# Retention and top-1 MoE on one core: expert 0's rows transposed inside the last retention tiles, expert 1's weight splits on two engines, its x transposed later, x loads tied to TensorE

## The chip, the core and the metric

The kernel runs on one core of one Trainium2 chip. The metric is the device time of one execution in microseconds (us). Runs of the kernel before: 649.43 us median of 3 (648.3 to 650.15).

Engines are called PE (TensorE; PEld is its weight load), DVE (VectorE), ACT (ScalarE), POOL (GpSimd) and SP (SyncE, which here only issues DMAs). "Clock" is the granted TensorE clock as a share of full speed.

## The reference

```python
# attention: 8 batches, 8 heads, 576 positions, head size 64
scores = (q @ k.T) / sqrt(64)
ret = scores * Dmat               # gamma_h ** (i - j) for i >= j, else 0; no softmax
x = (ret @ v)                     # -> [4608, 512], one row per token
# mixture of experts, top 1 of 8, F = 1024
logits = x @ w_gate
e_idx = argmax(logits, axis=1)
gate_w = softmax(logits)[e_idx]
eom = sigmoid(x @ w_output_gate)
for e in range(8):
    rows = e_idx == e
    h = relu(x[rows] @ w1[e])     # [., 512] @ [512, 1024]
    out[rows] = gate_w[rows] * eom[rows, e] * (h @ w2[e])
```

## The kernel before

**Phase 1, the retention.** 36 tiles of 128 tokens (`NTILE`), g = 0 to 35. Per tile PE makes the scores (L317), transposes k (`k_rows`, PSUM tile `k_ps`, L300), turns the last tile's result into row blocks with the gate logits (`xnat`, L437, tiles `xa`, `xb`), makes the tile's output (`outT`, L348 and L351, tile `o_ps`) and updates the state (`update`, L333, tile `st_ps`). DVE masks the scores (L319), adds the logits (L448, L449) and scales the output into `xT` (L355). Every fourth tile the gate runs: `gate1` on DVE (argmax, softmax, counts), `gate2` on PE (ranks, L394, L395), `gate3` on DVE (slots). Then POOL scatters the rows by indirect DMA into a DRAM buffer `xs` with a region for each expert (L185), and fills the unused slots of each region (`fill`, from `zx`). During this phase the weights of expert 0 are loaded (`start_w`), rounded by ACT (`hi_w`, L137) and the remainder taken by DVE (`lo_w`, L142) by the table `wsched`. Every operand of the MoE is split into such a high and a low part, and a product is three matmuls: high with high, high with low, low with high.

**Phase 2, the experts.** Each expert has 616 slots: part 0 with 360 (tiles 0 to 2, of 128, 128 and 104 rows) and part 1 with 256 (tiles 3 and 4, starting at slot 360). `mm1(e, part, fb)` makes one of eight h groups of a part: 12 matmuls (L237) into `h_ps`, of 360 or 256 columns, then ACT's `hh` (L239) and DVE's `hl` (L240). `mm2(e, t)` makes one tile of y: 24 matmuls (L253), then ACT's scaled copy (L256) and POOL's indirect store (L257). Expert 0 runs part 0 first as a whole (all h groups, then y of tiles 0 to 2) and then part 1; the other experts interleave the two parts group by group.

**How x reaches PE.** Expert 0's tiles 0 to 2 are loaded as rows (`load_rows`, one DMA of 2 KB rows, tile `x_g`) at g = 32 and transposed on PE (`transp`, L218) into `h_ps` after the retention. All other tiles are loaded by `load_x` (four DMAs of 128 pieces of 512 bytes, tile `x_q`, five buffers) and transposed in blocks by DVE (L221, tile `x_t`). In both cases ACT then rounds (`xh`, L223) and DVE takes the remainder (`xl`, L224). Every read of `xs` waits for all scatters and fills that were issued ahead of it in the program (`scat`, in `read`, L154).

**What sets the order.** The program is written in a fixed order (`manual_schedule`), and each engine runs its instructions in that order. Between the phases only PE, ACT, DVE and SP are fixed (`every`, L473, L510). SP has one queue, for all loads of weights, x and indices. From expert 1 on, the weights are split by DVE alone (`load_w`, L146 and L147); for expert 1 this happens during expert 0's part 1, where DVE also transposes expert 1's tiles 1 and 2; tile 0 is done ahead of it, tiles 3 and 4 with the last two y groups. The short POOL memsets on `gap` stand between scatters.

Of the kernel before, what the change touches and what calls it, by code (L numbers as in the profile page):

```python
# [47 lines left out]
def tile_retention_moe(  # L48
# [101 lines left out]
    XG, XT, HT = {}, {}, {}  # L150
    scat, todo, at = [], [], {}
    pools = {"xt0": xta, "ht0": hpa}

    def read(**kw):  # L154
        i = SP.dma_start(**kw)
        for j in scat:
            tc.add_manual_dep(i.ins, j.name, SYNC, reason="reads the rows after every scatter so far")
        tc.add_to_no_dep_group("xs", i.ins)
# [6 lines left out]
    def load_x(e, t):  # L165

        XG[e, t] = pools["xq"].tile([P, 4, P], F32, name="x_q")
        o = e * NT + ROW0[t]
        for a in range(4):
            read(out=XG[e, t][32 * a:32 * a + 32],  # L170
                 in_=xs[o:o + P, P * a:P * a + P].rearrange("(u j) c -> j u c", u=4))
# [35 lines left out]
    def transp(e, t):  # L207
# [7 lines left out]
        if e == 0 and part == 0:  # L215
            src = pools["ps_h"].tile([P, KB, P], F32, name="h_ps")[:, :, 0:m]
            for k in range(KB):
                T.transpose(src[:, k, :], XG[e, t][0:m, k:DM:KB], ident[0:m, 0:m])  # L218
        else:
            src = pools["xq"].tile([P, KB, P], F32, name="x_t", bufs=2)  # L220
            V.transpose(out=src.rearrange("p k (u j) -> p u k j", u=4),  # L221
                        in_=XG[e, t].rearrange("p u (i k) -> p u k i", k=KB))
# [3 lines left out]
    def mm1(e, part, fb):  # L226
# [8 lines left out]
        for k in range(KB):  # L235
            for a, b in ((wh, xh), (wh, xl), (wl, xh)):
                T.matmul(ps, lhsT=a[:, k, :], rhs=b[:, k, 0:n], start=(j == 0), stop=(j == 3 * KB - 1))  # L237
                j += 1
# [3 lines left out]
    def mm2(e, t):  # L242
# [6 lines left out]
        for fb in range(FB):  # L249
            wh, wl = (a[:, fb % 2, :] for a in W2[e, fb // 2])  # L250
            hh, hl = HT[e, part, fb]
            for a, b in ((hh, wh), (hh, wl), (hl, wh)):
                T.matmul(ps, lhsT=a[:, n], rhs=b, start=(j == 0), stop=(j == 3 * FB - 1))  # L253
                j += 1
# [217 lines left out]
    gap = const.tile([1, 1], F32, name="gap")  # L472
    every = {mybir.EngineType.PE, mybir.EngineType.Activation, mybir.EngineType.DVE, mybir.EngineType.SP}  # L473
    with tc.manual_schedule():
        S_next = scores(0)
        k_rows(0)
        for g in range(NTILE):
# [13 lines left out]
            if g + 1 < NTILE:  # L491
                prep(g + 1)
                S_next = scores(g + 1)
                k_rows(g + 1)
            if todo and g >= GT * SNAP + 10:
# [5 lines left out]
            update(g)  # L501
            if g % GT == 0 and g > 0:
# [8 lines left out]
    rest.__enter__()  # L511
    xnat(NTILE - 1)
    gate1(NTILE // GT - 1)
    for t in range(TA):
        transp(0, t)
# [50 lines left out]
    mm1(0, 0, 0)  # L566
# [12 lines left out]
    mm1(0, 0, 1)  # L579
    rest.__exit__(None, None, None)  # L580
    gap_ = gap

    def fill_slots(e):
        for f in fills[e]:
            G.memset(gap_, 0.0)
# [3 lines left out]
    for t in range(TA, CT):  # L589
        load_x(0, t)  # L590
    load_idx(0, 1)
    fill_slots(1)
    for t in range(3):
        load_x(1, t)
    load_idx(1, 0)
    load_idx(1, 1)
    fill_slots(2)
    for fb in range(2, FB):
        mm1(0, 0, fb)
    for t in range(TA):  # L600
        mm2(0, t)
        if t < CT - TA:
            transp(0, TA + t)
        else:
            transp(1, 0)
    for e in range(E):
        nx = e + 1 < E
        for fb in range(FB):
# [5 lines left out]
            if nx:  # L614
                if fb < CT if e else fb in (2, 3):
                    load_x(e + 1, fb if e else fb + 1)
                if e and fb in (5, 6):
# [3 lines left out]
            if fb == 7 and e + 3 < E:  # L621
                fill_slots(e + 3)
            if e == 0 and fb in (2, 6):
                transp(1, 1 if fb == 2 else 2)
        if e == E - 1:
            overflow_table()
        for t in range(CT):
            if e > 0 or t >= TA:
                if nx:
                    transp(e + 1, t)  # L630
# [99 lines left out]
```

## Time and profile before

| what | before |
|---|---|
| runs, median of 3 | 649.43 us (648.3 to 650.15) |
| the profiled execution, its time | 650.73 us |
| its span, from the first to the last instruction | 648.9 us |
| mean granted clock over the span | 0.982 |
| PE busy | 621.5 us (96%) |
| DVE busy | 358.7 us (55%) |
| ACT busy | 170.8 us (26%) |
| POOL busy | 166.9 us (26%) |
| bytes moved by DMA | 96.24 MB, mean 148 GB/s |

A row of the profile names the line of the kernel, the engine and the operation, then output and inputs by the program's names, then the shape and the count. In a view by time the first two numbers are the start and the duration in us; the brackets at the end hold the engine's idle time ahead of the instruction and what ended it. In a view by stretch each engine's busy time stands with its count of instructions, then the clock, the share of the DMA engines' time and the rate in GB/s. A busy PE is not PE at its peak: matmuls are pipelined, and their ends are modelled.

### The profile page before, as it was taken

To read this page: it belongs to the slowest core of one execution; us is meant where nothing else is said; L and a number is where in the kernel's file an instruction comes from. 1 tells how busy PE (TensorE), PEld (TensorE's weight loads), DVE (VectorE), ACT (ScalarE), POOL (GpSimd) and SP (SyncE) were. 2 spreads that over 40 slices of the span, in tenths; PEclk is the share of its full clock that TensorE was granted. 3 is DMA by queue.
4 is the path that set the end of the run, shared out by engine and by line. 5 is a ranking of instruction groups with operands and counts; after the bars stand their busy time and mean duration, and the time that the engine had idled before them with its cause. 6 is when DMAs were issued, how large, how long until landed. Compare 5 with 4: busy or idle time off the path is not lost. (4 is left out here: it accounts for less than half of the span.)

```text
span 648.9 us, 12779 instructions
## 1 busy us (share of the span) xinstructions
PE 621.5 (96%) x5127; PEld 551.9 (85%) x5127; DVE 358.7 (55%) x750; ACT 170.8 (26%) x379; POOL 166.9 (26%) x229
## 2 busy tenths in 40 slices
PE   8999999989969699999999999999999999999995
PEld 6888888878859488997997898799799889979974
DVE  3567787677753237773575286267438518625420
ACT  2333433323431122222222222222222222222210
POOL 2244433545426441401501320150110110010011
PEclk9999999989989699999999999999999999999999
DMA  9867686656424545633364183254417416311001
GB/s 323 275 232 251 219 292 231 215 197 240 147 90 129 141 138 162 188 106 127 115 178 130 59 235 88 82 151 117 143 62 212 126 36 186 123 46 65 0 34 43
DMA packets 55610, 96.24 MB, mean 148 GB/s; under 512 B 14736, under 2 KB 36625, under 8 KB 55548
## 3 DMA queue, kind: packets, MB, share of 16 engines
q1 hardware_dynamic: 45836, 72.99, 37.1%
q0 software_dynamic: 9280, 21.36, 9.0%
q10 hardware_dynamic: 432, 1.05, 0.4%
q8 instruction: 41, 0.67, 0.4%
q14 instruction: 21, 0.17, 0.1%
HBM read 74.02 MB, written 30.64 MB: 161 GB/s over the span
## 5 line engine op out<-in xcount | busy, mean ns | idle before, releaser
L237 PE MATMUL h_ps<-xh,w1h 128*128 128x360 f32 (+1 forms) x512 | 157.1, 307 | 2.9 <-ACT xh L223 2.5
L237 PE MATMUL h_ps<-xl,w1h 128*128 128x360 f32 (+1 forms) x512 | 157.0, 307 | 0.3 <-DVE xl L224 0.3
L237 PE MATMUL h_ps<-xh,w1l 128*128 128x360 f32 (+1 forms) x512 | 156.9, 306 | 0.0
L253 PE MATMUL y_ps<-w2h,hh 128*128 128x512 f32 (+1 forms) x320 | 127.2, 397 | 4.8 <-ACT hh L239 4.8
L257 POOL DMA_INDIRECT out_dram<-y,idx x40 | 39.7, 994 | 346.8 <-ACT y L256 333.8
L253 PE MATMUL y_ps<-w2h,hl 128*128 128x512 f32 (+1 forms) x320 | 126.4, 395 | 1.5 <-issue 1.5
L253 PE MATMUL y_ps<-w2l,hh 128*128 128x512 f32 (+1 forms) x320 | 126.4, 395 | 0.0
L240 DVE SCALAR_TENSOR_TENSOR hl<-h_ps,hh 128x360 fp32r<-128x360 f32 (+1 forms) x128 | 58.7, 475 | 101.1 <-ACT hh L239 99.3
L237 PEld LDWEIGHTS h_ps<-xh,w1h 128*128 128x128 f32 x512 | 97.7, 191 | 3.6 <-ACT xh L223 2.7
L239 ACT ACTIVATE hh<-h_ps 128x360 fp32r<-128x360 f32 (+1 forms) x128 | 54.9, 429 | 171.0 <-PE h_ps L237 151.1
L237 PEld LDWEIGHTS h_ps<-xl,w1h 128*128 128x128 f32 x512 | 97.7, 191 | 1.0 <-DVE xl L224 0.7
L237 PEld LDWEIGHTS h_ps<-xh,w1l 128*128 128x128 f32 x512 | 97.5, 190 | 0.0
L253 PEld LDWEIGHTS y_ps<-w2h,hh 128*128 128x128 f32 (+1 forms) x320 | 59.5, 186 | 20.6 <-ACT hh L239 6.2
L224 DVE TENSOR_TENSOR xl<-x_t,xh 128x512 fp32r<-128x512 f32 x37 | 25.6, 692 | 91.1 <-ACT xh L223 90.4
L253 PEld LDWEIGHTS y_ps<-w2h,hl 128*128 128x128 f32 (+1 forms) x320 | 59.5, 186 | 16.5 <-issue 1.3
L253 PEld LDWEIGHTS y_ps<-w2l,hh 128*128 128x128 f32 (+1 forms) x320 | 59.5, 186 | 14.4
L256 ACT ACTIVATE y<-y_ps,idx 128x512 f32<-128x512 f32 (+1 forms) x40 | 27.6, 690 | 146.7 <-issue 77.2
L319 DVE TENSOR_TENSOR S_sb<-sc,cmat_sb 128x512 f32<-128x512 f32 x72 | 46.1, 682 | 17.9 <-PE sc L317 17.9
L185 POOL DMA_INDIRECT xs<-xgrp,sli x36 | 38.3, 1063 | 66.8 <-ACT xgrp L443 20.9
L306 POOL TENSOR_TENSOR vp<-pk,gk_sb 128x512 f32<-128x512 f32 x36 | 37.6, 1044 | 54.0 <-PE st_ps L333 40.5
L185 POOL DMA_INDIRECT xs<-zx,fill x40 | 47.2, 1180 | 9.5 <-issue 9.4
L317 PE MATMUL sc<-pk 64*128 64x128 f32 x576 | 43.7, 289 | 1.8 <-DVE S_sb L319 1.5
(116 smaller groups left out, 669.9 us busy)
## 6 DMA issues: line engine op xcount, KB each, us to landing
st<-in_w_dram SPq DMA_DIRECT2D x64, 512.0 KB
pk<-in_pack_dram SPq DMA_DIRECT2D x32, 768.0 KB
x_q<-xs SPq DMA_DIRECT2D x148, 64.0 KB
gq_sb<-in_gq_dram SPq DMA_DIRECT2D x5, 256.0 KB
pk<-in_pack_dram SPq DMA_DIRECT2D x4, 256.0 KB
pk<-in_pack_dram SPq DMA_DIRECT2D x2, 512.0 KB
xs<-zx,fill POOLq DMA_INDIRECT x40
out_dram<-y,idx POOLq DMA_INDIRECT x40
```

The lines of the kernel that those rows point to most:

```text
L185: i = G.indirect_dma_start(out=xs, out_offset=bass.IndirectOffsetOnAxis(ap=at, axis=0), in_=x, in_offset=None, **({} if bound is None else ...
L224: V.tensor_tensor(out=lo, in0=src, in1=hi.bitcast(F32), op=ALU.subtract)
L237: T.matmul(ps, lhsT=a[:, k, :], rhs=b[:, k, 0:n], start=(j == 0), stop=(j == 3 * KB - 1))
L239: A.activation(out=hh, in_=ps, func=AF.Relu)
L240: V.scalar_tensor_tensor(out=hl, in0=ps, scalar=0.0, in1=hh.bitcast(F32), op0=ALU.max, op1=ALU.subtract)
L253: T.matmul(ps, lhsT=a[:, n], rhs=b, start=(j == 0), stop=(j == 3 * FB - 1))
L256: A.activation(out=y, in_=ps, func=AF.Copy, scale=idx.bitcast(F32)[0:m, e, t, 1:2])
L257: G.indirect_dma_start(out=out, out_offset=bass.IndirectOffsetOnAxis(ap=idx[0:m, e, t, 0:1], axis=0), in_=y, in_offset=None, bounds_check= ...
L306: G.tensor_tensor(out=vs[g], in0=pk[g][:, 2].rearrange("p (h d) -> p h d", h=H), in1=gk_sb[:, g % CPB].broadcast_to([P, H, D]), op=ALU.mult)
L317: T.matmul(sc[r][:, p], lhsT=k, rhs=q, start=True, stop=True)
L319: V.tensor_tensor(out=S_sb[:, r], in0=sc[r], in1=m, op=ALU.mult)
```

## The change

- `transp` for expert 0 uses PE for all five tiles, into a PSUM tile that `pools["ps_x"]` names: `k_ps` in the retention, `t_ps` later. Tiles 0 and 1 are transposed in iterations g = 34 and 35, after `scores(g + 1)` and ahead of `xnat(g - 1)`, tile 2 after the last `outT`.
- `mm1(0, 0, 0)` goes ahead of `xnat(35)` and the last `gate1`, and `mm1(0, 0, 1)` ahead of `gate2`.
- Expert 0's tiles 3 and 4 are loaded as rows, and transposed on PE between y of tile 1 and y of tile 2.
- Expert 1's first weights: the loads of quarters 0 and 1 are issued right after expert 0's last x, those of 2 and 3 in part 1; the split is ACT's `hi_w` and DVE's `lo_w` in two halves each instead of DVE alone.
- Expert 1's x: tile 0 is loaded behind y of tile 1, tile 1 behind the transposes and y of tile 2, tiles 2 to 4 at h groups 1, 3 and 5 of part 1. The first DMA of each also waits for the first matmul of the group that was last written in the program (`pe[0]`). All five are transposed at the end: 0 to 2 ahead of y of tile 3, 3 and 4 ahead of y of tile 4.
- The slot fills of expert 2 move from the start of phase 2 into part 1 of expert 0, the later ones from three experts ahead to two.

```diff
+    pe = [None]
-    def read(**kw):
+    def read(paced=False, **kw):
         i = SP.dma_start(**kw)
+        if paced:
+            tc.add_manual_dep(i.ins, pe[0].name, SYNC, reason="not before TensorE is at this point")
...
-            read(out=XG[e, t][32 * a:32 * a + 32],
+            read(paced=e == 1 and a == 0, out=XG[e, t][32 * a:32 * a + 32],
...
-        if e == 0 and part == 0:
-            src = pools["ps_h"].tile([P, KB, P], F32, name="h_ps")[:, :, 0:m]
+        if e == 0:
+            src = pools["ps_x"].tile([P, KB, P], F32, name=pools["x_ps"])[:, :, 0:m]
...
+            if g >= NTILE - 2:
+                transp(0, g - NTILE + 2)
...
             update(g)
+            if g == NTILE - 1:
+                transp(0, 2)
...
+    mm1(0, 0, 0)
     xnat(NTILE - 1)
     gate1(NTILE // GT - 1)
-    for t in range(TA):
-        transp(0, t)
...
-    mm1(0, 0, 0)
+    pools["ps_x"], pools["x_ps"] = ps_t, "t_ps"
+    mm1(0, 0, 1)
     gate2(ps_t.tile([P, 512], F32, name="t_ps"), True)
...
-    mm1(0, 0, 1)
...
     for t in range(TA, CT):
-        load_x(0, t)
+        load_rows(0, t)
     load_idx(0, 1)
+    w = [start_w(1, 1, fp) for fp in range(2)]
     fill_slots(1)
-    for t in range(3):
-        load_x(1, t)
+    for fb in range(2, FB):
+        mm1(0, 0, fb)
     load_idx(1, 0)
     load_idx(1, 1)
-    fill_slots(2)
-    for fb in range(2, FB):
-        mm1(0, 0, fb)
-    for t in range(TA):
-        mm2(0, t)
-        if t < CT - TA:
-            transp(0, TA + t)
-        else:
-            transp(1, 0)
+    mm2(0, 0)
+    mm2(0, 1)
+    load_x(1, 0)
+    for t in range(TA, CT):
+        transp(0, t)
+    mm2(0, 2)
+    load_x(1, 1)
...
-            if nx:
-                if fb < CT if e else fb in (2, 3):
-                    load_x(e + 1, fb if e else fb + 1)
-                if e and fb in (5, 6):
+            if e == 0:
+
+                if fb in (0, 2):
+                    w.append(start_w(1, 1, 2 + fb // 2))
+                if fb in (1, 3, 5):
+                    load_x(1, 2 + fb // 2)
+                if fb % 2 == 1:
+                    hi_w(*w[fb // 2])
+                    lo_w(*w[fb // 2])
+            elif nx:
+                if fb < CT:
+                    load_x(e + 1, fb)
+                if fb in (5, 6):
...
-            if fb == 7 and e + 3 < E:
-                fill_slots(e + 3)
-            if e == 0 and fb in (2, 6):
-                transp(1, 1 if fb == 2 else 2)
+            if fb == (7 if e else 4) and e + 2 < E:
+                fill_slots(e + 2)
...
             if e > 0 or t >= TA:
-                if nx:
-                    transp(e + 1, t)
+                for u in (t,) if e else range(3) if t == TA else range(3, CT):
+                    if nx:
+                        transp(e + 1, u)
                 mm2(e, t)
```

On PE, at the end of the retention (state update of tile 34, row block, output of tile 35), the order was, with the numbers of buffers in the names:

```order
L333 MATMUL st_ps<-vp,kn 64x64 x8
L437 MATMUL xa<-iw,xT 128x144 x2
L437 MATMUL xb<-iw,xT 128x144 x2
L348 MATMUL o_ps<-pk,stT_95 64x128 x8
L351 MATMUL o_ps<-S_sb,vp 64x128 x8
L437 MATMUL xa<-iw,xT 128x144 x2
L437 MATMUL xb<-iw,xT 128x144 x2
L218 MATMUL h_ps<-cmat_sb,x_g 128x128 x8
L218 MATMUL h_ps<-cmat_sb,x_g 128x104 x4
L237 MATMUL h_ps<-xh_2797,w1h_572 128x360
```

At the same place the changed kernel has (its line numbers are higher by 3 to 12):

```order
L340 MATMUL st_ps<-vp,kn 64x64 x8
L221 MATMUL k_ps<-cmat_sb,x_g 128x128 x4
L444 MATMUL xa<-iw,xT 128x144 x2
L444 MATMUL xb<-iw,xT 128x144 x2
L355 MATMUL o_ps<-pk,stT_95 64x128 x8
L358 MATMUL o_ps<-S_sb,vp 64x128 x8
L221 MATMUL k_ps<-cmat_sb,x_g 128x104 x4
L240 MATMUL h_ps<-xh_2673,w1h_572 128x360
```

The transposes stand between the pieces of the last tiles, and the first h group follows the last output directly; the last `xa` and `xb` come after its 12 matmuls.

On SP, from the last weights of expert 0 on, the queue was:

```order
L128 DMA st<-in_w_dram 128x1024
L155 DMA x_q<-xs 32x4x128 x8
L155 DMA idx<-xs 128x2x2
L155 DMA x_q<-xs 32x4x128 x12
L155 DMA idx<-xs 128x3x2
L155 DMA idx<-xs 128x2x2
L128 DMA st<-in_w_dram 128x1024
L155 DMA x_q<-xs 32x4x128 x8
L128 DMA st<-in_w_dram 128x1024 x4
```

and it is now:

```order
L128 DMA st<-in_w_dram 128x1024
L156 DMA x_g<-xs 128x512 x2
L156 DMA idx<-xs 128x2x2
L128 DMA st<-in_w_dram 128x1024 x2
L156 DMA idx<-xs 128x3x2
L156 DMA idx<-xs 128x2x2
L156 DMA x_q<-xs 32x4x128 x8
L128 DMA st<-in_w_dram 128x1024
L156 DMA x_q<-xs 32x4x128 x4
L128 DMA st<-in_w_dram 128x1024
```

Two row loads stand in place of the first eight x pieces, two weight loads come ahead of expert 1's x, and the x pieces come by four with weights between them.

On DVE, at the end of expert 0's part 1 (the last h groups, then the border to expert 1), the order was:

```order
L221 STREAM_TRANSPOSE x_t<-x_q 128x4x4x32
L224 TENSOR_TENSOR xl_3193<-x_t,xh_3192 128x4x128
L240 SCALAR_TENSOR_TENSOR hl_3354<-h_ps,hh_3353 128x256
L146 CAST w1h_3372<-st 128x1024
L147 TENSOR_TENSOR w1l_3373<-st,w1h_3372 128x1024
L221 STREAM_TRANSPOSE x_t<-x_q 128x4x4x32
L224 TENSOR_TENSOR xl_3397<-x_t,xh_3396 128x4x128
L221 STREAM_TRANSPOSE x_t<-x_q 128x4x4x32
L224 TENSOR_TENSOR xl_3397<-x_t,xh_3396 128x4x128
```

and it is now:

```order
L245 SCALAR_TENSOR_TENSOR hl_3350<-h_ps,hh_3349 128x256
L142 TENSOR_TENSOR w1l_3242<-st,w1h_3241 128x512 x2
L224 STREAM_TRANSPOSE x_t<-x_q 128x4x4x32
L227 TENSOR_TENSOR xl_3371<-x_t,xh_3370 128x4x128
L224 STREAM_TRANSPOSE x_t<-x_q 128x4x4x32
L227 TENSOR_TENSOR xl_3371<-x_t,xh_3370 128x4x128
L224 STREAM_TRANSPOSE x_t<-x_q 128x4x4x32
L227 TENSOR_TENSOR xl_3371<-x_t,xh_3370 128x4x128
L224 STREAM_TRANSPOSE x_t<-x_q 128x4x4x32
L227 TENSOR_TENSOR xl_3415<-x_t,xh_3414 128x4x128
L224 STREAM_TRANSPOSE x_t<-x_q 128x4x4x32
L227 TENSOR_TENSOR xl_3415<-x_t,xh_3414 128x4x128
```

All five tiles of expert 1 (`xl_3371` is its part 0, `xl_3415` its part 1) now stand in one row behind the last weight split.

## Prediction before the run

> **What bounds the kernel now.** I read the page's busy line first, then busy time by stretch over the change of phase, then TensorE (PE) in order of time with the idle time ahead of each piece, then what released ScalarE (ACT) and VectorE (DVE) there.
>
> ```profile
> PE 621.5 (96%) x5127; PEld 551.9 (85%) x5127; DVE 358.7 (55%) x750; ACT 170.8 (26%) x379; POOL 166.9 (26%) x229
> ```
>
> PE is busy 96% of the span of 648.9 us, and the change takes no matmul away, so a gain can only come from its 27.4 us of idle time and from time at a reduced clock. The stretches (columns: us, then busy time of PE, PEld, DVE, ACT, POOL, then the granted clock) show where both lie:
>
> ```profile
> 182.40:185.80 3.40, 1.72 (x14) 1.75 (x15) 2.12 (x5) 0.75 (x2) 0.38 (x2) 1.00 0.30 113
> 185.80:189.30 3.50, 0.97 (x9) 0.80 (x8) 3.12 (x16) 1.81 (x5) 0.00 (x0) 1.00 0.01 2
> 189.30:196.10 6.80, 6.52 (x23) 5.87 (x24) 2.37 (x11) 1.50 (x3) 0.00 (x0) 0.50 0.00 0
> 196.10:208.70 12.60, 12.60 (x78) 12.60 (x77) 5.19 (x17) 2.36 (x5) 9.23 (x12) 1.00 0.43 147
> ...
> 213.10:216.60 3.50, 0.91 (x3) 0.48 (x3) 0.53 (x1) 0.47 (x1) 2.93 (x6) 1.00 0.76 182
> 216.60:226.80 10.20, 6.50 (x16) 4.84 (x16) 3.25 (x4) 1.67 (x3) 1.97 (x2) 0.50 0.57 148
> ```
>
> There are two holes: around 182 to 196 us (the last retention tile, the transposes of expert 0's rows, its first h groups) and 213 to 227 us (the first y group). Each is followed by a stretch at clock 0.50. PE in order of time, first hole:
>
> ```profile
> 178.81 0.73 PE L437 MATMUL xa<-iw,xT 128*128 128x144 f32 x4 [0.85 <-DVE xT L355]
> ...
> 180.56 1.09 PE L351 MATMUL o_ps<-S_sb,vp 128*64 128x128 f32 x16
> 184.08 0.73 PE L437 MATMUL xa<-iw,xT 128*128 128x144 f32 x4 [2.43 <-DVE xT L355]
> ...
> 185.14 1.58 PE L218 MATMUL h_ps<-cmat_sb,x_g 128*128 128x128 f32 x12
> 189.25 0.67 PE L237 MATMUL h_ps<-xh,w1h 128*128 128x360 f32 x1 [2.53 <-ACT xh L223]
> 190.20 0.67 PE L237 MATMUL h_ps<-xl,w1h 128*128 128x360 f32 x1 [0.28 <-DVE xl L224]
> ```
>
> Second hole, and its end where the first 256-column group starts:
>
> ```profile
> 206.62 0.33 PE L237 MATMUL h_ps<-xh,w1l 128*128 128x360 f32 x1
> ...
> 208.75 0.39 PE L253 MATMUL y_ps<-w2h,hh 128*128 128x512 f32 x1
> 214.14 0.50 PE L253 MATMUL y_ps<-w2h,hh 128*128 128x512 f32 x1 [1.05 <-ACT hh L239]
> 216.43 0.48 PE L253 MATMUL y_ps<-w2h,hl 128*128 128x512 f32 x1 [1.55 <-issue]
> 220.61 0.79 PE L253 MATMUL y_ps<-w2h,hh 128*128 128x512 f32 x1 [3.70 <-ACT hh L239]
> ```
> ```profile
> 235.33 0.28 PE L237 MATMUL h_ps<-xh,w1h 128*128 128x256 f32 x1
> ```
>
> In the second hole PE waits for hh of groups 6 and 7, which ACT makes late, and ACT itself says why:
>
> ```profile
> 213.62 0.47 ACT L239 ACTIVATE hh<-h_ps 128x360 fp32r<-128x360 f32 x1 [8.08 <-remote]
> 220.09 0.47 ACT L239 ACTIVATE hh<-h_ps 128x360 fp32r<-128x360 f32 x1 [6.00 <-remote]
> ```
>
> Group 6 ends on PE at 206.62 + 0.33 = 206.95, yet ACT, idle and waiting for PE alone, starts 6.7 us later; group 7 ends near 208.92 and is taken 11.2 us later. "Remote" says that the release was not tied to an instruction at that time. What ran meanwhile is on the queues: SyncE's reads of expert rows in 512-byte pieces.
>
> ```profile
> 206.04 4.40 SPq L155 DMA_DIRECT2D x_q<-xs  x8
> 210.49 0.43 SPq L155 DMA_DIRECT2D idx<-xs  x1
> 212.76 7.47 SPq L155 DMA_DIRECT2D x_q<-xs  x12
> ```
>
> Both late releases fall into these issues, the second at the end of the burst. That the burst holds them up is my reading, not a row.
>
> **Part A: the transposes move into the retention, one h group goes ahead of the last row block (PE).** Before, PE left the retention's last matmul at 180.56 + 1.09 = 181.65 and reached y at 208.75. After, on the same clock of time: VectorE gets one xl (0.6 us; the three of them take 1.78) ahead of xT(34), for which PE already waits (0.85), so the tail ends some 0.55 later, at 182.2; the other transposes there fill that wait. Then the third tile's transposes, 4 of the 12 that took 1.58: 0.5. Their cast and subtraction are now exposed: about 0.75 until xh and 0.45 until xl, 1.2. Then 8 h groups of 12 at 12.60/77 = 0.164 (the window's 78 hold one that began before): 15.7. The last row block, 184.08 to 185.14: 1.05. The rank matmuls and a short wait for DVE's counts: 0.5. Sum 182.2 + 0.5 + 1.2 + 15.7 + 1.05 + 0.5 = 201.2, so A = 208.75 - 201.2 = **7.55 us** saved. The new group 0 covers xT(35) and group 1 covers the gate's chain on DVE. Bounds: if DVE's xT(35) is released late again (2.43 idle in its row) and the clock halves again, 7.55 - 1.6 - 3.0 = 3; if the casts hide wholly, 8.7.
>
> **Part B: expert 0's last two tiles and expert 1's x.** The whole-row load of tiles 3 and 4 is 2 issues instead of 8, and expert 1's x no longer follows in the same burst: 12 of the 20 x_q issues wait for PE's first y groups or later. The last scatters move with the gate. Before (rows below), the rank matmuls came at 193.67, the first scatter at 197.17, the first read at 206.04. The rank matmuls now come after h group 1, at 182.2 + 0.5 + 1.2 + 2 x 1.97 + 1.05 = 188.9 or a little later, 4.5 earlier, so the reads come near 201.5, just after h group 7 has ended. So the late releases should go.
>
> ```profile
> 193.67 0.25 PE L394 MATMUL t_ps<-oh,cbf_sb 128*128 128x32 bf16 x1
> ```
> ```profile
> 197.17 1.26 POOL L185 DMA_INDIRECT xs<-xgrp,sli  x1 [14.39 <-issue]
> ```
>
> What is late next? The transposes of tiles 3 and 4, which PE meets after two y groups:
>
> ```profile
> 246.80:257.80 11.00, 11.00 (x50) 9.06 (x49) 8.77 (x12) 2.67 (x5) 0.98 (x1) 1.00 0.69 191
> ```
>
> That stretch holds two undisturbed y groups, 48 matmuls, and an h record at each edge: 10.97, or 0.2285 each. So PE is at the transposes at 201.2 + 10.97 = 212.2. The loads are 512 KB; at the 182 GB/s of the window 213.1 to 216.6 they take 2.9 us, at a third of it 8.6, so they are there by 204.4 to 210.1. Their cast and subtraction (1.2 and 1.4) lie under the third y group. B: before, 208.75 to 235.33 = 26.58; after, 72 x 0.2285 = 16.45 and 8 transposes at 1.58/12 = 0.13, 1.05. B = 26.58 - 17.5 = **9.1 us** saved, so PE is at the 256-column groups at 218.7. Bounds: 0 if the releases stay late, 10 if the transposes hide.
>
> **Part C: x of expert 1 after its weights (VectorE, then PE).** The weight splits themselves go from DVE alone (0.69 + 1.23 each) to ACT and DVE; per two 256-column groups ACT has 2 x 0.39 + 1.14 and DVE 2 x 0.42 + 1.28 of work in 2.88 us of PE, so both keep up. But all five tiles of x(1) are now transposed in one chain after the last split:
>
> ```profile
> 253.69 1.08 DVE L221 STREAM_TRANSPOSE x_t<-x_q 128x512 f32<-128x512 f32 x1
> 255.52 0.69 DVE L224 TENSOR_TENSOR xl<-x_t,xh 128x512 fp32r<-128x512 f32 x1 [0.74 <-ACT xh L223]
> 256.13 1.08 DVE L221 STREAM_TRANSPOSE x_t<-x_q 128x512 f32<-128x512 f32 x1
> ```
> ```profile
> 178.33 1.14 ACT L137 CAST w2h<-st 128x512 fp32r<-128x512 f32 x2
> ```
>
> One tile takes 256.13 - 253.69 = 2.44, since DVE waits for ACT's cast in between. Count from the end of the last 256-column group: hh 0.55, the last weight cast 1.14, the second half of its subtraction 0.7: the chain starts at 2.4. The fifth xl starts at 2.4 + 4 x 2.44 + 1.83 = 14.0 and ends at 14.7; its xh is there at 14.0. PE has 10.97 of y and 12 x 0.164 = 1.97 of h(1,0,0) until it needs tiles 3 and 4 at 12.94. Before, the last two tiles were done by 258.6, 11.75 after, so nothing waited. Now PE waits 1.05 for xh, does one matmul, and waits 0.6 for xl: C = **-1.7 us**. Bounds: 0 if the splits end earlier, -4 with a late x load. Which clock follows? In the window 182.4 to 185.8 PE was busy 1.72 of 3.4 and the clock stayed; here it is busy about 1.8 of 3.4, so I take no loss. Against that stands one row with more work than that and a halved clock behind it:
>
> ```profile
> 134.70:138.10 3.40, 1.93 (x36) 1.33 (x26) 3.36 (x6) 0.17 (x1) 3.20 (x5) 1.00 0.61 199
> 138.10:141.50 3.40, 3.40 (x21) 3.18 (x22) 2.06 (x4) 0.26 (x1) 1.07 (x3) 0.50 0.99 308
> ```
>
> That is 1.7 us more for one window at half rate, 3.4 for two.
>
> [...]
>
> **Moved at no cost.** The five slot fills of expert 2 leave the crowded time for the 256-column groups; POOL has nothing else there, and only the last x load of expert 1 waits for them. It would cost if they landed after the chain's fifth transpose.
>
> **Sum.** 7.55 + 9.1 - 1.7 = 14.95. The profiled execution took 650.73 (span 648.9 and 1.8 around it): 635.8. The runs' median is 649.43, 1.3 lower: 634.5. I take 635.0, with 632 to 639 for this case by the bounds near the middle.
>
> **Rivals.**
> - *The clock halves at the border to expert 1, or the chain there runs longer* (the row at 138.1 speaks for it, the one at 182.4 against): 1.7 to 3.4 more, 637 to 638.5. Chance 0.12.
> - *The transposes of tiles 3 and 4 wait for their load.* Before, the tile asked for at 206.04 was transposed on DVE only 15 us later (row below). If a whole-row load takes as long, it lands at 216.5, PE waits 4.3, and two half-rate windows cost 3.0: 635.0 + 7.3 = 642.5. Against it: no burst behind it in the queue. Chance 0.08.
>
> ```profile
> 221.04 1.09 DVE L221 STREAM_TRANSPOSE x_t<-x_q 128x512 f32<-128x512 f32 x1
> ```
>
> - *The late release comes again*, because the fills on POOL hold it up and not the x reads. Then B is -1.05 instead of 9.1: 645. Against it: group 5, like the ones before, was taken at once (204.64 + 0.33 = 204.97 on PE, by the 0.164 step back from group 6; 205.06 on ACT) while POOL scattered and filled from 197.17 on. Chance 0.07.
>
> ```profile
> 205.06 0.47 ACT L239 ACTIVATE hh<-h_ps 128x360 fp32r<-128x360 f32 x1 [1.56 <-PE h_ps L237]
> ```
>
> - *The slow stretches stay though the waits go*, because something else halves the clock there: the stretch at 189.3 costs 6.8 - 23 x 0.164 - 0.28 = 2.7, the other 6.50/2 = 3.25, so 6 less is gained: 641. Against it: each began right behind a window with PE busy for less than 1 of 3.5 us. Chance 0.03. [...]
> - *Slower than before: SyncE's one queue stands at a paced read.* Everything for expert 1 is now in one file on SyncE, each x tile behind a wait for PE. The third tile is released at 220.2 and wanted on DVE at 218.7 + 11.5 + 2.4 + 4.9 = 237.5; after 1.9 us of issue and 2 of landing its slack is 13.4. PE must be held 15 us longer than that to lose all that A and B save, so it decides from a release 28 us late. The latest seen is 11.2. It would give 651 and more. Chance 0.03.
>
> The forecast has 0.66; 0.01 is left for what I don't see. Within 632 and 643 lie most of the forecast's 0.66, and the border, load and clock rivals (0.23): about 0.83. A difference of 0.3%, 1.9 us, is about the least that a measurement of this kernel can tell from none. All but the last rival are faster by more: 0.95, same 0.02, slower 0.03.
>
> **What would show it.** Right: no wait of over 1.5 us between the last o_ps and the first y on PE, no half-rate stretch after it; hh of groups 6 and 7 within 0.5 us of their matmuls; the first 256-column h 16 to 17 us earlier, near 218.7; one wait of 1 to 2 us at the first h group of expert 1's second part, put down to ACT xh or DVE xl. Wrong: "remote" releases again at y, PE waiting for the load of x_g at the transposes, a half-rate stretch after the border, or a border wait of over 4 us.

## The result, and the profile after

| | before | after |
|---|---|---|
| runs of the comparison, median | 649.03 us (648.3 to 650.15) | 640.02 us (638.22 to 642.48) |
| ratio, 95% interval | | 0.9862 (0.9821 to 0.9904) |
| the profiled execution | 650.73 us, span 648.9, clock 0.982 | 642.48 us, span 640.5, clock 0.992 |

The change gained 9.0 us. The forecast was 635.0, range 632 to 643: the sign and the wide range held, the middle was 5 us too low, and the narrower 632 to 639 that the prediction gave for its own case did not hold. One thing has to be known ahead of the rest: the later runs were made on three chips (5, 10 and 12 on record; the comparison has no chip on record), and on two of them, 5 and 10, **the kernel before takes 638 us, not 649**. These two are called quiet below. On chip 5 the changed kernel takes 636.8, ratio 0.9979 (0.9964 to 0.9995). So most of the 9.0 us belongs to something that befell the kernel before in the comparison, and the experiments are about what that was.

Busy time of the changed kernel, from its page:

```profile
PE 619.3 (97%) x5135; PEld 550.2 (86%) x5135; DVE 354.0 (55%) x748; ACT 174.1 (27%) x387; POOL 167.2 (26%) x229
```

To compare the traces I cut each at five rows of PE: the scores of tile 35, the first y, the first 256-column h group, the first h group of expert 1, its first y. The stretches between them are the retention's tail, y of tiles 0 to 2, part 1 with y of tiles 3 and 4, and the h groups of expert 1. Columns: us, length, busy PE, PEld, DVE, ACT, POOL, clock, then DMA share and GB/s. Before, in the first comparison:

```profile
173.50:208.70 35.20, 29.10 (x235) 27.17 (x232) 19.24 (x66) 10.73 (x25) 15.26 (x21) 0.90 0.29 99
208.70:235.30 26.60, 20.30 (x74) 15.03 (x73) 5.48 (x7) 3.34 (x6) 9.31 (x17) 0.81 0.56 151
235.30:257.80 22.50, 22.50 (x145) 20.53 (x144) 16.90 (x24) 7.04 (x15) 8.28 (x12) 1.00 0.49 139
257.80:285.10 27.30, 27.30 (x194) 27.29 (x193) 19.98 (x30) 7.24 (x17) 7.34 (x11) 1.00 0.61 175
```

After, in the same comparison:

```profile
174.30:202.70 28.40, 26.91 (x234) 24.75 (x233) 19.55 (x67) 11.05 (x26) 12.04 (x15) 1.00 0.29 105
202.70:220.30 17.60, 17.60 (x82) 14.03 (x82) 1.82 (x3) 2.81 (x5) 7.16 (x11) 1.00 0.61 171
220.30:243.50 23.20, 22.52 (x145) 20.64 (x144) 13.29 (x23) 9.91 (x21) 6.39 (x12) 1.00 0.62 171
243.50:275.70 32.20, 29.49 (x193) 28.77 (x192) 22.50 (x33) 8.19 (x18) 7.34 (x12) 0.95 0.52 160
```

The first two stretches lost all their half-rate time and most of PE's idle time (6.1 and 6.3 before, 1.5 and none after): 35.2 - 28.4 = 6.8 and 26.6 - 17.6 = 9.0 are the gain. The last two gave back 0.8 and 5.0 (23.25 - 22.48 and 32.21 - 27.25, by the rows that the rounded cuts stand for). With 0.7 that the changed execution began later and 0.9 in experts 2 to 7 and the end, this is the 8.4 between the spans.

Where the 5.0 went stands on PE at the border to expert 1. It first waits for the fifth x cast, then for its remainder, and then runs at half rate:

```profile
247.45 0.38 PE L240 MATMUL h_ps<-xh,w1h 128*128 128x256 f32 x1 [1.84 <-ACT xh L226]
248.18 0.58 PE L240 MATMUL h_ps<-xl,w1h 128*128 128x256 f32 x1 [0.34 <-DVE xl L227]
```
```profile
244.70:248.10 3.40, 1.30 (x7) 0.81 (x5) 2.36 (x3) 1.64 (x4) 0.00 (x0) 1.00 0.23 89
248.10:251.50 3.40, 3.32 (x14) 3.33 (x15) 0.65 (x3) 0.63 (x2) 2.76 (x5) 0.50 0.32 119
```

And late releases are still there. ACT in order of time, with its idle time in brackets:

```profile
203.62 0.47 ACT L244 ACTIVATE hh<-h_ps 128x360 fp32r<-128x360 f32 x1 [2.24 <-PE h_ps L240]
210.97 0.69 ACT L263 ACTIVATE y<-y_ps,idx 128x512 f32<-128x512 f32 x1 [6.88 <-remote]
...
225.78 0.38 ACT L244 ACTIVATE hh<-h_ps 128x256 fp32r<-128x256 f32 x1 [1.02 <-PE h_ps L240]
230.16 0.39 ACT L244 ACTIVATE hh<-h_ps 128x256 fp32r<-128x256 f32 x1 [4.00 <-PE h_ps L240]
```
```profile
225.91 0.28 PE L240 MATMUL h_ps<-xh,w1l 128*128 128x256 f32 x1
```

The hh of group 6 is prompt now and that of group 7, at 203.62, is 0.8 behind PE (the prediction had asked for 0.5 of both), but the copy of the first y comes about 2.5 us late, and the hh at 230.16 belongs to a group that ended at 225.91 + 0.28 = 226.19: 4.0 late. PE does not need the y copy. The late hh it does feel: the casts and subtractions of ACT and DVE queue up behind it, and the row of five transposes starts 3.4 us behind the first y of tile 3 (232.62) instead of the 2.4 that the prediction had counted:

```profile
236.03 1.09 DVE L224 STREAM_TRANSPOSE x_t<-x_q 128x512 f32<-128x512 f32 x1
...
247.43 0.69 DVE L227 TENSOR_TENSOR xl<-x_t,xh 128x512 fp32r<-128x512 f32 x1 [0.68 <-ACT xh L226]
```

### The profile page after: what moved, and what is told of

It is laid out like the page before. It is cut to its first block, busy times and chain, and to the rows that moved or that the text cites. A ratio compares the mean times of both kernels' runs of the same rounds, so it can differ in the third digit from the quotient of the medians.

```text
span 640.5 us, 12798 instructions
## 1 busy us (share of the span) xinstructions
PE 619.3 (97%) x5135; PEld 550.2 (86%) x5135; DVE 354.0 (55%) x748; ACT 174.1 (27%) x387; POOL 167.2 (26%) x229
## 3 DMA queue, kind: packets, MB, share of 16 engines
q10 hardware_dynamic: 432, 1.05, 0.4%
## 5 line engine op out<-in xcount | busy, mean ns | idle before, releaser
L240 PE MATMUL h_ps<-xl,w1h 128*128 128x360 f32 (+1 forms) x512 | 156.7, 306 | 0.5 <-DVE xl L227 0.5
L258 PE MATMUL y_ps<-w2h,hh 128*128 128x512 f32 (+1 forms) x320 | 125.8, 393 | 0.0
L227 DVE TENSOR_TENSOR xl<-x_t,xh 128x512 fp32r<-128x512 f32 x35 | 24.2, 693 | 80.6 <-ACT xh L226 79.2
```

What stands on the lines that cost most here:

```text
L227: V.tensor_tensor(out=lo, in0=src, in1=hi.bitcast(F32), op=ALU.subtract)
L240: i = T.matmul(ps, lhsT=a[:, k, :], rhs=b[:, k, 0:n], start=(j == 0), stop=(j == 3 * KB - 1))
L258: i = T.matmul(ps, lhsT=a[:, n], rhs=b, start=(j == 0), stop=(j == 3 * FB - 1))
```

## The experiments

Theory at the start: PE's releases are held up by the bursts of 512-byte reads (with POOL's fills beside them); the change broke the bursts up, and what is left of them delays the row of transposes and so makes the border's loss. Rivals: the fills alone; something that is not in the program; the border's loss has another cause.

The first four ran together, on chip 5. **after_again** is the changed kernel itself.

> The changed kernel once more, as the base for the next three on the same chip, and to see which of its losses are there in a second profile. Theory (chain too long behind a late release): the hh of part 1's group 3 is again taken 3 to 4 us late, the row of five x transposes starts 3.4 us behind the last 256-column group, PE waits 2 us at the first h group of expert 1's part 1, and the clock is halved behind it; 640 us, ratio 0.986. Rival (the loss at the border belongs to the one profiled execution, which was the slowest of four): no such wait here, 638 us.

Measured: 636.8 us, and the kernel before beside it 637.98; ratio 0.9979 (0.9964 to 0.9995). Neither side had expected that of the kernel before. Its stretches, cut as above:

```profile
172.30:200.10 27.80, 26.61 (x234) 24.46 (x233) 19.63 (x67) 11.03 (x26) 11.93 (x15) 1.00 0.30 107
200.10:217.70 17.60, 17.60 (x82) 14.03 (x81) 1.82 (x3) 2.81 (x5) 7.24 (x12) 1.00 0.61 182
217.70:240.10 22.40, 22.40 (x146) 20.51 (x145) 14.37 (x23) 10.50 (x22) 7.62 (x12) 1.00 0.62 185
240.10:269.20 29.10, 27.95 (x194) 27.30 (x193) 21.57 (x32) 8.01 (x18) 7.36 (x11) 1.00 0.54 164
```

No late hh, no half rate. The row of transposes starts at 231.57, 2.4 behind y of tile 3 (229.18), and PE's wait at the border is half of what it was:

```profile
231.57 1.08 DVE L224 STREAM_TRANSPOSE x_t<-x_q 128x512 f32<-128x512 f32 x1
```
```profile
242.98 0.38 PE L240 MATMUL h_ps<-xh,w1h 128*128 128x256 f32 x1 [0.81 <-ACT xh L226]
243.70 0.39 PE L240 MATMUL h_ps<-xl,w1h 128*128 128x256 f32 x1 [0.34 <-DVE xl L227]
```

**tile0_early** takes one tile out of the row:

```diff
     load_x(1, 1)
+    transp(1, 0)
     for e in range(E):
...
-                for u in (t,) if e else range(3) if t == TA else range(3, CT):
+                for u in (t,) if e else range(1, 3) if t == TA else range(3, CT):
```

> Of expert 1's five x transposes one (tile 0) goes ahead of expert 0's part 1, so four are left in the row behind the last weight split. Theory (the length of the row sets the border wait, and the wait the half-rate stretch): the last xl comes 2.4 us earlier, PE waits under 0.5 us at the border, no half-rate stretch; 2.2 of wait and 1.7 of half rate are saved: 636 us, ratio 0.980. Rival (the clock halves there for another reason, or the row simply starts later): the half-rate stretch stays, at most 2 us saved, 638 us or more.

Measured: 634.7 us, 0.9949 (0.993 to 0.9968), against 0.9979 of after_again: 0.3% or 1.9 us better. The h groups of expert 1 now run without a gap:

```profile
242.20:269.50 27.30, 27.30 (x194) 27.25 (x193) 19.93 (x30) 7.37 (x17) 7.37 (x11) 1.00 0.56 167
```

27.3 instead of 29.1: with one tile less in the row the wait is gone. The half rate, which I had counted in, was not there to be saved.

**fills_early** and **x_late** were to tell fills from reads as the cause of the late hh in part 1.

```diff
     fill_slots(1)
+    fill_slots(2)
...
-            if fb == (7 if e else 4) and e + 2 < E:
+            if fb == 7 and 0 < e < E - 2:
```

> The fills of expert 2 go back to where they were before, right behind expert 1's, so that POOL fills alone from 200 to 216 us, with no read in 512-byte pieces beside them until 214; in expert 0's part 1 no fill is left. Theory (late releases need fills and 512-byte reads together): hh of groups 6 and 7 within 1 us of their matmuls, and no late hh in part 1, where only reads are left; 0.95 of wait and about 1 at the border saved: 638 us. Rival 1 (fills alone hold the releases up): hh of 6 and 7 come 6 us late as in the kernel before, 645 us or more. Rival 2 (the 512-byte reads alone): the late hh near 226 us stays, 640 us.

```diff
-                if fb in (1, 3, 5):
-                    load_x(1, 2 + fb // 2)
+                for t in {1: (2,), 7: (3, 4)}.get(fb, ()):
+                    load_x(1, t)
```

> Expert 1's x tiles 3 and 4 are loaded behind the last h group of expert 0's part 1 instead of at its groups 3 and 5; the fills of expert 2 stay at group 4. Theory (fills and 512-byte reads together): no late hh near 226 us, as the fills now stand alone there; the row of transposes starts 1 us earlier; 638 us. Rival (fills alone, or something else at that point): the late hh stays, 640 us; if the loads now come too late for the fourth and fifth transposes, the border wait grows beyond 2 us.

Measured: 636.68 us, 0.9974 (0.9956 to 0.9991), and 636.62 us, 0.9976 (0.9958 to 0.9995). Both like after_again, with the same 0.81 at the border. Since this chip shows no late release in after_again either, the two tell nothing about the cause.

The next four ran on chip 10, with the kernel before at 637.75. **tail_only** is part A alone: the changed tail of the retention, and phase 2 as before (`load_x` for expert 0's tiles 3 and 4, `load_w` for expert 1, its x transposed as before).

```diff
...
-        if e == 0:
+        if e == 0 and part == 0:
             src = pools["ps_x"].tile([P, KB, P], F32, name=pools["x_ps"])[:, :, 0:m]
...
     for t in range(TA, CT):
-        load_rows(0, t)
+        load_x(0, t)
...
```

> Part A alone: the new tail of the retention (transposes inside the last tiles, two h groups earlier); loads, fills, weight splits and x transposes of phase 2 as before. Theory 1 (the two parts add): y starts 6.8 us earlier, the late hh of groups 6 and 7 and the half-rate stretch behind them stay: 649.0 - 6.8 = 642 us. Theory 2 (the late releases hang on the first x_q burst, which starts by POOL's scatters and not by PE): groups 6 and 7 now end before the burst, so part A alone brings most of part B too, without the border's loss: 634 to 637 us.

**phase2_only** is the rest: parts B and C with the old tail.

```diff
-            if g >= NTILE - 2:
-                transp(0, g - NTILE + 2)
...
-    mm1(0, 0, 0)
     xnat(NTILE - 1)
     gate1(NTILE // GT - 1)
+    pools["ps_x"], pools["x_ps"] = ps_h, "h_ps"
+    for t in range(TA):
+        transp(0, t)
...
```

> Parts B and C alone: the retention's tail as before, loads, fills, weight splits and x transposes as changed. Theory (512-byte reads held the releases up): hh of groups 6 and 7 within 1 us, no half-rate stretch in y; 9.0 saved in y, 0.8 and 5.0 lost in part 1 and at the border: 646 us. Rival (fills on POOL hold them up): hh of groups 6 and 7 late again, and the border's loss comes on top: 650 us or more.

Measured: tail_only 632.05 us, 0.9912 (0.988 to 0.9943); phase2_only 641.78 us, 1.0061 (1.0041 to 1.008). Part A alone gains more than the whole change did on chip 5, and parts B and C alone are slower than the kernel before. Neither number of the theories is met, as both counted with late releases, and the traces show none.

**before_fills_late** holds the ten fills back in the kernel before, so that the first reads stand alone.

```diff
...
         for f in fills[e]:
-            G.memset(gap_, 0.0)
+            i = G.memset(gap_, 0.0)
+            if e == 1:
+                tc.add_manual_dep(i.ins, pe[0].name, SYNC, reason="not before TensorE is at this point")
...
-    fill_slots(1)
-    for t in range(3):
-        load_x(1, t)
-    load_idx(1, 0)
-    load_idx(1, 1)
-    fill_slots(2)
...
+        if t == 1:
+            fill_slots(1)
+            for u in range(3):
+                load_x(1, u)
+            load_idx(1, 0)
+            load_idx(1, 1)
+            fill_slots(2)
...
-            if e == 0 and fb in (2, 6):
-                transp(1, 1 if fb == 2 else 2)
+            if e == 0 and fb in (3, 5, 7):
+                transp(1, fb // 2 - 1)
```

> The kernel before, with the ten fills of experts 1 and 2, and expert 1's first three x tiles behind the first five, held back until the first matmul of y of tile 1; the first eight 512-byte reads (expert 0's tiles 3 and 4) stay where they were, now with no fill beside them. Theory (fills and reads together, or fills alone): hh of groups 6 and 7 within 1 us of their matmuls; the hole of some 9 us with its half-rate stretch goes or moves into y, where it holds nothing up: 642 us. Rival (the reads alone hold the releases up): hh of group 6 comes 4 us late or more beside the eight reads: 647 us or more.

Measured: 653.77 us, 1.0237 (1.0207 to 1.0267). The hh are prompt, but without a late release in the kernel before that says nothing. The time is lost elsewhere: x of expert 1 now lands too late, its transposes stand in DVE's queue ahead of hl, and PE waits there:

```profile
245.30 0.58 PE L238 MATMUL h_ps<-xh,w1h 128*128 128x256 f32 x1 [11.20 <-DVE hl L241]
```

**fetch_shift** adds 32 short matmuls to the warm-up.

```diff
+    z16 = zx.bitcast(BF16)
+    for n in range(32):
+        T.matmul(warm[:, 0:32], lhsT=z16[:, 0:P], rhs=z16[:, 0:32], start=True, stop=True)
     prep(0)
```

> The changed kernel with 32 short bf16 matmuls more in the warm-up ahead of the first scores, so that PE's own instruction fetches (16 KB each in the trace, one for 128 matmuls) come 32 matmuls earlier. Theory (PE's late releases come where such a fetch meets other traffic): the late hh of part 1 moves from 226 towards 222 us, to wherever the fetch now is, or goes. Rival (fills and 512-byte reads alone set the place): it stays at group 3, 226 us from the start, less what the start shifts.

Measured: 637.17 us in one run, no late hh: inconclusive, for the same reason.

Then the kernel before itself, with a profile, and part A again (**before_again**, unchanged, and **tail_again**, the edit of tail_only).

> The kernel before once more, with a profile, since it took 637.8 us in the experiments so far and 649.0 in the comparison. Theory 1 (the late releases of PE were a state of the first occasion, not of the program): if it takes 638 us, its hh of groups 6 and 7 are taken within 1 us, PE has no wait over 1 us in y of expert 0 and no half-rate stretch there; what is left of the old hole is the retention's tail, with xh and xT waits of 1 to 3 us. Theory 2 (the late releases are there every time, and the 11 us come from elsewhere, the clock or a load): hh of groups 6 and 7 again 6 us late or more.

> Part A alone once more, beside a profile of the kernel before on the same chip. Theory 1 (no late releases in this state, parts B and C only cost): 5 to 7 us below the kernel before, 632 us, and PE without a wait over 0.5 us from the first h group to expert 1's end. Theory 2 (late releases back, before at 649): A's own 6.8 and whatever of the hole lies behind the first read: between 634 and 642 us.

Measured: before_again 637.2 us. Run in the place of the changed kernel it reads 0.9978 (0.9956 to 0.9999) against itself, so 0.2% is not to be read as a difference here. tail_again 633.78 us, 0.9935 (0.9906 to 0.9963). The profile of before_again decides the first theory. ACT at groups 6 and 7, then SP's reads and the first and last of POOL's fills beside them:

```profile
203.49 0.47 ACT L239 ACTIVATE hh<-h_ps 128x360 fp32r<-128x360 f32 x1 [1.50 <-PE h_ps L237]
205.47 0.47 ACT L239 ACTIVATE hh<-h_ps 128x360 fp32r<-128x360 f32 x1 [1.50 <-PE h_ps L237]
```
```profile
203.59 4.76 SPq L155 DMA_DIRECT2D x_q<-xs  x8
...
210.44 5.56 SPq L155 DMA_DIRECT2D x_q<-xs  x12
```
```profile
203.98 0.99 POOL L185 DMA_INDIRECT xs<-zx,fill  x1 [0.24 <-issue]
...
214.30 0.99 POOL L185 DMA_INDIRECT xs<-zx,fill  x1 [0.24 <-DMA x_q<-xs]
```

The same 20 reads and the same fills at the same place of the program, and each hh follows its group as all the others do. Its stretches:

```profile
174.20:205.30 31.10, 26.32 (x236) 24.64 (x233) 19.76 (x67) 11.17 (x26) 14.27 (x20) 1.00 0.30 107
205.30:221.90 16.60, 16.60 (x73) 13.00 (x72) 5.03 (x6) 2.86 (x5) 10.24 (x17) 1.00 0.65 160
221.90:244.60 22.70, 22.70 (x145) 20.43 (x144) 17.24 (x24) 6.82 (x15) 8.75 (x12) 1.00 0.64 204
244.60:271.90 27.30, 27.30 (x193) 27.23 (x193) 19.94 (x30) 7.35 (x17) 7.21 (x11) 1.00 0.60 175
```

There is no hole in y to be closed: PE is busy for the whole 16.6 us. So the reads, with the fills, do not suffice to hold a release up.

The last two ran on chip 12, where the kernel before took 649.74 us again. **chain_late** is the changed kernel with the row of transposes 1 us later.

```diff
+                if e == 0 and t == TA:
+                    d = pools["xq"].tile([P, KB, P], F32, name="x_t", bufs=2)
+                    V.transpose(out=d.rearrange("p k (u j) -> p u k j", u=4),
+                                in_=XG[1, 0].rearrange("p u (i k) -> p u k i", k=KB))
                 for u in (t,) if e else range(3) if t == TA else range(3, CT):
```

> The changed kernel with one x transpose of 1.08 us more on DVE, into a spare buffer, ahead of the row of five, so that the row starts 1.0 us later, as a late release made it start in the first profile. Theory (the border's loss is the row's lateness, and the clock follows PE's wait): PE waits 1.8 and 0.3 us at the first h of part 1 instead of 0.8 and 0.3, and the clock is halved for one stretch of 3.4 us behind it: 1.0 and 1.7 more than the changed kernel, 639.5 us where that takes 636.8. Rival (the half-rate stretch at the border belonged to the first occasion, as the late releases did): 1.0 us more and no half rate, 637.8 us.

Measured: 638.9 us, 0.9829 (0.9797 to 0.9861). The added transpose and the first of the five on DVE, then PE at the border, the two windows there, and the whole stretch:

```profile
234.09 1.08 DVE L647 STREAM_TRANSPOSE x_t<-x_q 128x512 f32<-128x512 f32 x1
235.09 1.04 DVE L224 STREAM_TRANSPOSE x_t<-x_q 128x512 f32<-128x512 f32 x1
```
```profile
246.45 0.38 PE L240 MATMUL h_ps<-xh,w1h 128*128 128x256 f32 x1 [1.86 <-ACT xh L226]
247.18 0.38 PE L240 MATMUL h_ps<-xl,w1h 128*128 128x256 f32 x1 [0.34 <-DVE xl L227]
```
```profile
245.20:248.60 3.40, 1.81 (x13) 1.61 (x14) 1.77 (x3) 1.57 (x3) 1.09 (x3) 1.00 0.00 0
248.60:252.00 3.40, 3.40 (x14) 3.40 (x13) 2.25 (x3) 0.38 (x1) 2.90 (x5) 0.50 0.42 153
```

```profile
242.50:274.00 31.50, 29.29 (x194) 28.80 (x193) 22.57 (x33) 8.19 (x18) 7.80 (x12) 0.95 0.52 161
```

The comparison is with after_again, on another chip. This trace has late releases too (the hh of part 1's group 3 is taken at 227.57, after 2.71 idle), but by the border they cost the row only 0.1: the added transpose starts 2.49 behind the first y of tile 3 (231.60), where the row of after_again starts 2.39 behind. A row that starts 1.1 later makes the wait 1.86 instead of 0.81, and the clock halves behind it; the h groups of expert 1 take 31.5 instead of 29.1, 2.4 more, of which 1.05 is the wait and some 1.3 the half rate. The border's wait is the row's lateness, whatever makes it late; whether a half-rate window comes on top hangs on where the window's edges fall as well (last section).

**x_256** is the kernel before with twice as many, smaller reads.

```diff
+        n = 64 if e < 2 else P
         for a in range(4):
-            read(out=XG[e, t][32 * a:32 * a + 32],
-                 in_=xs[o:o + P, P * a:P * a + P].rearrange("(u j) c -> j u c", u=4))
+            for c in range(0, P, n):
+                read(out=XG[e, t][32 * a:32 * a + 32, :, c:c + n],
+                     in_=xs[o:o + P, P * a + c:P * a + c + n].rearrange("(u j) c -> j u c", u=4))
```

> The kernel before with the x reads of experts 0 and 1 in 256-byte pieces, so twice as many issues and pieces for the same bytes, beside the same fills. Theory (the reads in small pieces hold PE's releases up from some load on): hh of groups 6 and 7 more than 1 us behind their matmuls, a wait in y and a half-rate stretch as in the first profile: 645 us or more. Rival (their number is not what held them up): both hh within 0.5 us, PE without a wait in y; the loads end later, so DVE's transposes of tiles 3 and 4 may hold PE at the first 256-column group: 638 to 643 us.

Measured: 650.8 us, 1.0021 (1.0003 to 1.004). On this chip the kernel before is late as it is, and doubling the reads makes it no later by more than 0.2%. PE's last matmul of group 6, ACT's hh of groups 6 and 7, and the first read:

```profile
204.12 0.33 PE L239 MATMUL h_ps<-xh,w1l 128*128 128x360 f32 x1
```
```profile
207.22 0.47 ACT L241 ACTIVATE hh<-h_ps 128x360 fp32r<-128x360 f32 x1 [4.24 <-PE h_ps L239]
218.63 0.47 ACT L241 ACTIVATE hh<-h_ps 128x360 fp32r<-128x360 f32 x1 [10.94 <-remote]
```
```profile
204.60 9.67 SPq L155 DMA_DIRECT2D x_q<-xs  x16
```

Group 6 ended at 204.45, and its hh came 2.8 late. The first read was issued at 204.60, only 0.15 behind the group's end, so these rows don't say whether the delay began without the reads. An earlier one does: xT(35), which PE waits for at the end of the retention. PE's row here, then in before_again (in before the wait is 2.43):

```profile
182.73 0.73 PE L439 MATMUL xa<-iw,xT 128*128 128x144 f32 x4 [2.40 <-DVE xT L357]
```
```profile
183.24 0.73 PE L437 MATMUL xa<-iw,xT 128*128 128x144 f32 x4 [0.89 <-DVE xT L355]
```

That xT is 1.5 late in before and here, and in both the first x_q read is more than 20 us away, and the nearest fills 18 us or more (156.7 and 202.5 in before); POOL's last scatter of the retention is beside it, as in before_again. So a release can be late with neither reads nor fills beside it.

What does go with the late releases in every trace is that it holds fewer semaphore events. Their numbers in the traces, by whose semaphore it is (before and before_again are one program, after and after_again another; x_256 has more issues than before):

| trace | time of the kernel before beside it | PE | DVE | ACT | POOL |
|---|---|---|---|---|---|
| before | 649.0 | 516 | 697 | 358 | 97 |
| after | 649.0 | 517 | 692 | 358 | 97 |
| chain_late | 649.7 | 516 | 687 | 358 | 99 |
| x_256 | 649.7 | 512 | 695 | 350 | 93 |
| before_again | 638.2 | 528 | 732 | 368 | 111 |
| after_again | 638.0 | 530 | 729 | 375 | 111 |
| the other eight | 637.8 to 638.2 | 527 to 530 | 729 to 732 | 366 to 376 | 111 |

The instruction rows are all there (PE has 5127 in before and in before_again), but where releases are late, about an eighth of POOL's events (93 to 99 are there, against 111) and some of each other engine's are not. The events that are left put the delay on the side of the release: in before, PE's next event behind 205.04 stands at 213.59, 0.03 ahead of ACT's late hh, and in after three events of PE that after_again has at 205.56, 205.79 and 206.03 stand bunched at 210.87, 210.90 and 210.94, just ahead of the late y copy. Why there are fewer, and whether the same thing holds the releases up, no run here shows. Every run on record comes with a span and a granted clock, so none shows these times without recording, and whether the recording itself holds the engines up stays an untested rival.

## Why the prediction was right or wrong

- **Part A** (7.55 forecast, 3 to 8.7). Measured 6.8 in the comparison, and the row count was right: transposes in the wait, one xh exposed, y at 202.68 - 0.7 = 201.9 by the old clock against 201.2. But 31.1 - 27.8 = 3.3 is what the traces of before_again and after_again leave, without late releases. The other 3.5 were the late xT (2.43 against 0.89 in before_again) and the half-rate stretch behind it, less 0.6 that late releases cost the changed tail. So the step that failed is the old tail's end: I took its 2.43 and its half rate for the program's own. My lower bound of 3 comes near the 3.3 by luck: it took off the same two prices, but for the changed tail being late, not for the old one being prompt. And 3.3 is not the whole worth of A on a quiet chip: in before_fills_late, on chip 10, the same old tail has no late xT but a half-rate stretch, and takes 33.4 (last section), which would make it 5.6.
- **Part B** (9.1 forecast, 0 to 10). The size held, 9.0; the step under it, "that the burst holds them up is my reading", fell. The burst is neither enough (before_again) nor needed (the late xT(35) ahead of all reads in before and x_256, and the late y copy at 210.97 in after, with only whole-row reads, weights and POOL's fills near it). The reads didn't come as early as counted, either: the first was issued at 205.00, 204.3 by the old clock, and not near 201.5. Where nothing is late, part B costs 17.6 - 16.6 = 1.0, the eight PE transposes, which I had at 1.05. The row that could have warned me was in my own fence: PE's wait of 2.43 for xT(35) at 184.08, a late release with no x_q read in sight.
- **Part C** (-1.7 forecast, 0 to -4). Without late releases it is -1.8 (29.1 - 27.3), with the row at 2.4 behind the last group, as counted. In the comparison it was -5.0, beyond the bound. Two steps failed: "the late releases should go" (one came back at group 3 of part 1 and made the row 1.0 later), and "I take no loss" for the clock. The window at 182.4 had 1.72 busy and no halving; the window at the border had 1.30 busy. The first rival, a half rate at the border, came true on top of it. Two of the four signs that I had named for being wrong were there, a "remote" release at y (210.97) and the half-rate stretch behind the border, although the time lay in the range.
- **At no cost** I had put part 1: it lost 0.8 to the wait of PE behind the same late hh.
- **The rest of the 6.5** between 14.95 and the 8.4 of the spans is what I could not see: a start that was 0.7 later, and 0.9 over experts 2 to 7 and the end. Two runs of one kernel differ by as much; the one profiled was the slowest of four.
- **The rivals.** The clock rival (about 6 us less) fell: no half-rate stretch is left where the waits went (clock 1.00 from 174.3 to 243.5 in after). The late releases did come again, but not at the place that I priced. The transposes of tiles 3 and 4 did not wait for their load, as PE has no idle time in 202.70 to 220.30 (that rival's sum is 642.3, not the 642.5 that I wrote). SP's queue never mattered: x of expert 1's third tile was issued at 222.02 and wanted at 240.86.

So the time was right for the comparison, and for a reason that is only half in the program; that part B's size held without its cause is luck. On the quiet chips the whole change is worth 3.3 - 1.0 + 0.3 - 1.8, about 1 us by the traces, which the measurement cannot tell from none, and its first part alone is worth four to six by its ratios (0.9912 and 0.9935), which fits the 3.3 and 5.6 of the tail. On the quiet chips tail_only gained most against the kernel before; whether it also escapes late releases was not tried where they occur.

## What to carry to other kernels

When a wait is put down to a release that comes long after its matmul, ask first whether the program or the occasion made it: profile the same kernel again on another chip before you price its removal. Price a row of work that feeds the next stage from both of its ends, its length and when it can start: here a start 1.1 later made PE's wait 1.05 longer, and one tile less, 2.4 of work, took the wait of 0.8 and 0.3 away. And what counts in such a wait is also the window of the clock that it falls into, since one microsecond more brought 1.3 of half rate with it.

## What the runs showed of the hardware

- **The clock's windows lie on a grid.** In before and in after every change of the granted clock falls on one grid of 3.413 us for that execution: in before, 138.1 to 189.3 is 15 steps, 189.3 to 216.6 is 8; in after, 138.9 to 248.1 is 32. The grid lies elsewhere in the span in each execution: the first half-rate window starts at 138.08 in before and at 138.91 in after. The half-rate stretches shown of before_fills_late (188.9 to 195.7) and chain_late (248.6 to 252.0) are two steps and one. I counted PE's busy time in each window between the start and the end of the matmuls (the views' cuts, at tenths, shift a count by up to 0.1). Of the windows at full clock, those with 0.88 and 0.89 us busy (before), 1.28 (after) and 1.35 (before_fills_late) are followed by a half-rate window; the one with 1.97 (before_again) is not, nor is any with 2.28 or more in before and after. In between both occur: the clock halved behind 1.95 (before and after) and 1.81 (chain_late), and stayed behind 1.78 (before and before_again). Behind a window at half rate it can go either way: one with 3.13 busy (189.28 in before) was followed by another, one with 3.36 (248.13 in after) was not. The same wait can therefore cost a half-rate window or not, by where it falls: before_again has the gap of 2.52 us ahead of its first h group cut in two by the grid, and keeps its clock (PE's row, then the two windows):

```profile
188.40 0.43 PE L237 MATMUL h_ps<-xh,w1h 128*128 128x360 f32 x1 [2.52 <-ACT xh L223]
```
```profile
184.10:187.50 3.40, 1.78 (x15) 1.61 (x14) 2.59 (x16) 1.60 (x6) 0.00 (x0) 1.00 0.17 65
187.50:190.90 3.40, 1.97 (x10) 1.73 (x11) 1.81 (x4) 0.85 (x2) 0.00 (x0) 1.00 0.00 0
```

  In before_fills_late, whose retention and first h groups are the same program on the same chip, the same gap falls into one window, and the clock halves (PE's row, that window, the half-rate stretch):

```profile
189.37 0.67 PE L238 MATMUL h_ps<-xh,w1h 128*128 128x360 f32 x1 [2.52 <-ACT xh L224]
```
```profile
185.50:188.90 3.40, 1.35 (x12) 1.18 (x10) 2.71 (x16) 1.72 (x6) 0.00 (x0) 1.00 0.06 18
188.90:195.70 6.80, 6.04 (x21) 5.39 (x22) 2.43 (x8) 1.91 (x5) 0.00 (x0) 0.50 0.00 0
```

  From the scores of tile 35 to the first y this takes 33.4 us (175.22 to 208.65), against 31.0 in before_again: 2.4 more, with the same gap, where the clock halved. What makes the clock halve is not shown beyond these counts.
- **Late releases come with fewer event records, and by chip or occasion.** The same kernel takes 638 us on chips 5 and 10 and 649 on chip 12 and in the comparison, whose chip is not on record, so that chip and occasion can't be told apart. The instruction rows are the same (PE has 5127 in before and in before_again), the events fewer (POOL has 97 and 111). The 11 us are late releases in a few places, from 1.5 us (xT(35)) to 11.2 us (hh of group 7) in before, and the half-rate windows behind them (189.3 to 196.1 and 216.6 to 226.8). The cause stays open.
